# One attention step per FFN tile held back behind `p_packed @ w_in` in a fused attention and softplus-FFN kernel

## The chip, the core and the metric

The kernel runs on one core of one Trainium2 chip. The metric is the device time of one execution in microseconds (us), lower is better; a verdict rests on the median of several executions. The core has a matmul engine (PE, with its weight loads shown as PEld), VectorE (DVE), ScalarE (ACT), GpSimd (POOL) and a queue that issues transfers (SyncE, SP). Each works through its own instruction list, and they wait for one another by semaphores.

## The reference

Two attentions in a row for 8 batches and 8 heads, then an FFN over the 4608 tokens. `p` has 32 rows for each head, so the second attention has only 32 keys.

```python
def sm_attn(qq, kk, vv):
    s = scale * np.matmul(qq, kk.transpose(0, 1, 3, 2))
    s = s - np.max(s, axis=-1, keepdims=True)
    a = np.exp(s)
    a = a / (np.sum(a, axis=-1, keepdims=True) + 1e-09)
    return np.matmul(a, vv)
p_packed = sm_attn(p, k, v)
out = sm_attn(q, p_packed, p_packed)
...
h = x @ w_in
g = np.maximum(h, 0.0) + np.log1p(np.exp(-np.abs(h)))
return (g @ w_out).astype(np.float32)
```

Here batch and heads are 8 and 8, the sequence is 576, the head size 64, `w_in` is 512 x 2048 and `w_out` 2048 x 512. `x` is `out` with the heads side by side.

## The kernel before

Since `x` is (attention weights) @ `p_packed`, the kernel never forms `x`. It multiplies `p_packed` by `w_in` first (`make_m`, L535) and then applies the attention weights to that product (`gemm1`, L564). For each batch b the FFN runs over 16 **tiles** f of 128 columns of `d_ff`. Both FFN products are made from a high and a low half of each operand, in three matmuls (L579, L617).

The main loop (L717) takes one (b, f) at a time:

- `gemm1` of tile f: twelve matmuls (L580) into the two PSUM buffers `ph`;
- the softplus of tile f, spread out by a generator: on ACT the absolute value (L602), Exp (L604) and Ln (L605), on DVE max plus add (L607), which is what frees `ph` for the next `gemm1`, then the split into halves (L594, L595);
- `gemm2` of tile f - 2 (L618): four **token tiles** t = 0 to 3, three matmuls each, into the `acc` buffers;
- behind each token tile, steps of the attention of batch b + 1. A running sum `due` grows by `PACE` = 0.56 (0.62 in batch 1), and one step is made for each whole unit;
- in batch 0 only, also behind each token tile, pieces of a **conversion** that turns the 64-bit weights into 32 bits. One conversion is two ACT instructions (L200, L204), two on DVE (L206, L211) and an addition on POOL (L219); for `w_out` also a cast on ACT (L238) and a subtraction on DVE (L244);
- at the end of the tile, where the tile after next begins a new block of columns, `make_m` of that block: small matmuls (L543) into two PSUM banks `psm`, which ACT (L558) and DVE (L559) read out. A block is 256 columns in batch 0 (every second tile) and 512 in the other batches (every fourth).

The attention steps and `make_m` take their banks from the same pool, `ps_m`, which has two buffers used in turn. An attention step that writes a bank just ahead of `make_m` makes one of the two `psm` banks wait until that step's result is copied out: by L268 for a transposed piece of k or q (`transposed`, L257), by L309 for transposed attention weights (`a1_transposed`, L304). The first attention of the two first batches (`attention_first`, L370) transposes k and q on PE; from batch 2 on (`attention_next`, L445) DVE does it.

PE's instructions run in the order in which the code issues them. On ACT, DVE, POOL and SP the order is chosen by a scheduler when the program is built, from dependencies, priorities and estimated times; at run time each list is fixed.

```python
    PACE = 0.56
    ...
    PACE_FIRST = 0.62
```

Of the kernel before, what the change touches and what calls it, by code (L numbers as in the profile page):

```python
# [26 lines left out]
def pack_attention_then_softplus_ffn(  # L27
# [14 lines left out]
    P = 128  # L42
# [7 lines left out]
    NT = S // P  # L50
# [44 lines left out]
    def load_pack(bg, queues):  # L95

        t = cv.tile([PW, H, D], F32, tag="m", name=f"p_{bg}", bufs=1)
        for i in range(BG):
            queues[i % len(queues)].dma_start(
                t[i * J:(i + 1) * J], p[bg * BG + i].rearrange("h j d -> j h d")  # L100
            )
        return t

    def pack_transposed(bg, t):
        for o in range(0, H, HG):
            ps = bank(f"ppt_{bg}_{o}")
            for i in range(HG):
                nc.tensor.transpose(
                    ps[:D, i * PW:(i + 1) * PW], t[:, o + i, :], ident[:PW, :PW]
                )  # L110
            dst = pT[:, o:o + HG, :].rearrange("x h j -> x (h j)")
            nc.vector.tensor_copy(dst[:D], ps[:D, :HG * PW])
            nc.scalar.copy(dst[D:], ps[:D, :HG * PW])
# [401 lines left out]
    def attention(b):  # L515
        return attention_first(b) if b < FIRST else attention_next(b)

    def weights(b):

        at_h = work.tile([P, G, S], F32R, tag="at_h", name=f"at_h_{b}", bufs=1)  # L520
        at_l = work.tile([P, G, S], F32R, tag="at_l", name=f"at_l_{b}", bufs=1)
        res[b]["at"] = (at_h, at_l)
        for g in range(G):
            aT = res[b]["aT"][g]
            nc.scalar.copy(at_h[:, g, :], aT)  # L525
            nc.vector.tensor_tensor(  # L526
                at_l[:, g, :], aT, at_h[:, g, :].bitcast(F32), op=ALU.subtract
            )


    def m_cols(b):

        return MC if b else MC // 2
# [30 lines left out]
    def gemm1(b, f, res):  # L564

        n = m_cols(b)
        halves = res["m"][f * P // n]
        at_h, at_l = res["at"]
        phs = []
        for c in range(2):  # L570
            ph = ps_h.tile([P, 512], F32, tag="h", name=f"ph_{b}_{f}_{c}")
            phs.append(ph[:, :C])
            i = 0
            for g in range(G):
                mh, ml = halves[g * n // MC]
                o = g * n % MC + f * P % n
                ms = slice(o, o + P)
                cs = slice(c * C, (c + 1) * C)
                for x, y in ((mh, at_h), (mh, at_l), (ml, at_h)):  # L579
                    nc.tensor.matmul(  # L580
                        ph[:, :C], x[:, ms], y[:, g, cs],
                        start=(i == 0), stop=(i == 3 * G - 1),
                    )
                    i += 1
        return phs
# [11 lines left out]
    def softplus(b, f, hv, done):  # L597
        e = work.tile([P, S], F32, tag="e", name=f"e_{b}_{f}")
        es = [e[:, c * C:(c + 1) * C] for c in range(2)]
        spans = [e] if b == 0 else es  # L600
        for c in range(2):
            nc.scalar.activation(es[c], hv[c], AF.Abs)  # L602
            for x in spans[c:c + 1] if b else spans[:c]:
                nc.scalar.activation(x, x, AF.Exp, scale=-1.0)  # L604
                nc.scalar.activation(x, x, AF.Ln, bias=1.0)  # L605
        for c in range(2):
            nc.vector.scalar_tensor_tensor(es[c], hv[c], 0.0, es[c], op0=ALU.max, op1=ALU.add)  # L607
        yield
        yield
        r = (b % 2) * REST  # L610
        nc.gpsimd.tensor_copy(rest[:, rest_at(b, f), r:r + REST], e[:, NT * P:])  # L611
        yield
        done[b, f] = halves(f"{b}_{f}")
        split(*done[b, f], e[:, :NT * P])

    def gemm2_tile(acc, gh, gl, f, cs, first, last):
        for i, (x, y) in enumerate(((gh, wo_h), (gh, wo_l), (gl, wo_h))):  # L617
            nc.tensor.matmul(  # L618
                acc, x[:, cs], y[:, f, :],
                start=(first and i == 0), stop=(last and i == 2),  # L620
            )
# [73 lines left out]
    due = 0.0  # L695
# [19 lines left out]
    units = [(b, f) for b in range(B) for f in range(NF)]  # L715
    ahead, chain, due = iter(()), iter(()), 0.0
    for u in range(len(units) + LAG):  # L717
        if u < len(units):
            b, f = units[u]
            if f == 0:  # L720
                if (b + 1) % BG == 0 and b + 1 < B:
                    pack_transposed((b + 1) // BG, pt)
                ahead = attention(b + 1) if b + 1 < B else iter(())
                due = 0.0
            chain = softplus(b, f, gemm1(b, f, res[b]), gs)
            next(chain)
            if f == NF - 1:
                if (b + 2) % BG == 0 and b + 2 < B:
                    pt = load_pack((b + 2) // BG, (nc.sync,))
                for _ in ahead:  # L730
                    pass
                if b + 1 < B:
                    weights(b + 1)
        if u >= LAG:
            b2, f2 = units[u - LAG]
            gh, gl = gs.pop((b2, f2))
            if f2 == 0:
                acc = [ps_acc.tile([P, DM], F32, tag="acc", name=f"acc_{b2}_{t}") for t in range(NT)]
        last = u >= LAG and f2 == NF - 1 and b2 % 2 == 1
        if last:  # L740
            both = rests(b2)
            next(both)
        for t in range(NT):
            if u >= LAG:
                gemm2_tile(
                    acc[t], gh, gl, f2, slice(t * P, (t + 1) * P), f2 == 0, f2 == NF - 1
                )
                if f2 == NF - 1:
                    store(acc[t], [(0, b2, t * P, P)], f"{b2}_{t}", t)
            if u < len(units):  # L750
                due += PACE if b != FIRST - 1 else PACE_FIRST
                while due >= 1:
                    next(ahead, None)
                    due -= 1
                if b == 0:
                    cdue += CONV
                    while cdue >= 1:
                        next(conv, None)
                        cdue -= 1
            next(chain, None)  # L760
        if last:
            next(both)
        if u + 2 < len(units):


            nb, c = units[u + 2][0], units[u + 2][1] * P
            if c % m_cols(nb) == 0:
                make_m(nb, c // m_cols(nb), res[nb])
# [29 lines left out]
```

## Time and profile before

| what | value |
|---|---|
| median of 3 runs | 773.94 us (773.31 to 775.29) |
| the profiled execution | 774.48 us |
| its span in the trace | 772.7 us |
| PE busy | 729.3 us (94%), granted clock 0.985 on average |
| DVE busy | 527.4 us (68%) |
| ACT busy | 435.3 us (56%) |
| POOL busy | 99.0 us (13%) |

The three executions lie within 0.3% of one another. The profiled one lasted 1.8 us longer than its span, and 0.54 us longer than the median of the three. Busy time is the union of an engine's instructions; rows of the trace give a start, a duration, the engine, the source line, what is written and read, and in brackets how long the engine had stood still and what ended that.

### The profile page before, as it was taken

The page shows a single profiled execution, that of the slowest core. Times are in us where ns is not written, and L with a number is a line of the kernel's source. Part 1 is how long each engine was busy: PE and PEld are TensorE (multiplying, and loading weights), DVE is VectorE, ACT ScalarE, POOL GpSimd, SP SyncE. Part 2 cuts the span into 40 slices and gives each one's busy share as a digit, 9 for nine tenths or more (in the row PEclk, how much of TensorE's full clock was granted, in tenths as well). Part 3 has the DMA queues.
Part 4 walks back from the last instruction along what each step waited for, and adds up shares of the span by engine and source line. Part 5 has one row for each costly group of instructions (what it writes and reads, how often), then busy time and mean ns, then how long its engine had stood idle before and what let it go on. Part 6 is the DMA issues. An engine that isn't in the chain of part 4 may idle for free.

```text
span 772.7 us, 14153 instructions
## 1 busy us (share of the span) xinstructions
PE 729.3 (94%) x5360; PEld 577.0 (75%) x5360; DVE 527.4 (68%) x1092; ACT 435.3 (56%) x1057; POOL 99.0 (13%) x166
## 2 busy tenths in 40 slices
PE   6457997999999999999999999999999999999997
PEld 4346675687788778877887777878787777888886
DVE  2697869975877559575877559576877558565554
ACT  5667977666455445565555455565555355555540
POOL 1253434200000000000010000000010000000110
PEclk9969999999999999999999999999999999999999
DMA  9977644534302342052402332043401400010002
GB/s 205 247 194 179 180 133 125 120 74 78 76 17 68 63 68 57 1 116 47 87 0 69 62 63 62 1 98 51 92 1 55 75 2 1 1 55 1 1 1 68
DMA packets 149668, 55.97 MB, mean 72 GB/s; under 512 B 116320, under 2 KB 142944, under 8 KB 149600
## 3 DMA queue, kind: packets, MB, share of 16 engines
q1 hardware_dynamic: 149328, 55.00, 31.9%
q8 instruction: 42, 0.69, 0.4%
q14 instruction: 26, 0.21, 0.1%
q10 hardware_dynamic: 272, 0.07, 0.0%
HBM read 45.61 MB, written 9.44 MB: 71 GB/s over the span
## 4 chain that ended last, share of the span: by engine, by line
PE 82%; DVE 6%; ACT 6%; DMA 4%; POOL 1%; issue 1%; SPq 0%; ACTq 0%; DVEq 0%; POOLq 0%
PE acc L618 41%; PE ph L580 26%; PE acc_m L618 6%; PE psm L543 4%; PE ps L275 2%; DMA w_in_sb<-in_q 2%; PE psp L318 1%; PE psa L308 1%; DMA k<-in_k 1%; ACT m L200 1%; DVE at_l L526 1%; DVE t L211 1%; POOL t L219 1%; ACT e L604 1%; DVE t L206 1%
## 5 line engine op out<-in xcount | busy, mean ns | idle before, releaser
L602 ACT ACTIVATE e<-ph 128x288 f32<-128x288 f32 x256 | 103.1, 404 | 189.3 <-PE ph L580 142.4
L618 PE MATMUL acc<-wo_h,gh 128*128 128x512 f32 x512 | 207.6, 405 | 0.0
L607 DVE SCALAR_TENSOR_TENSOR e<-ph,e 128x288 f32<-128x288 f32 x256 | 113.3, 451 | 131.9 <-ACT e L605 128.2
L618 PE MATMUL acc<-wo_l,gh 128*128 128x512 f32 x512 | 200.9, 392 | 0.0
L618 PE MATMUL acc<-wo_h,gl 128*128 128x512 f32 x512 | 200.8, 392 | 0.0
L580 PE MATMUL ph<-at_h,mh 128*128 128x288 f32 x512 | 158.9, 310 | 14.8 <-ACT at_h L525 7.5
L580 PE MATMUL ph<-at_l,mh 128*128 128x288 f32 x512 | 153.3, 299 | 3.7 <-DVE at_l L526 3.7
L580 PE MATMUL ph<-at_h,ml 128*128 128x288 f32 x512 | 152.7, 298 | 0.0
L580 PEld LDWEIGHTS ph<-at_h,mh 128*128 128x128 f32 x512 | 97.6, 191 | 48.8 <-DVE e L607 10.8
L611 POOL COPY rest<-e 128x64 f32<-128x64 f32 x128 | 53.2, 416 | 575.8 <-DVE e L607 544.2
L618 PEld LDWEIGHTS acc<-wo_h,gh 128*128 128x128 f32 x512 | 96.2, 188 | 27.4 <-issue 10.2
L618 PEld LDWEIGHTS acc<-wo_h,gl 128*128 128x128 f32 x512 | 96.1, 188 | 21.0
L604 ACT ACTIVATE e<-e 128x288 f32<-128x288 f32 (+1 forms) x240 | 109.5, 456 | 3.9
L605 ACT ACTIVATE e<-e 128x288 f32<-128x288 f32 (+1 forms) x240 | 109.4, 456 | 3.2
L618 PEld LDWEIGHTS acc<-wo_l,gh 128*128 128x128 f32 x512 | 96.4, 188 | 13.0
L580 PEld LDWEIGHTS ph<-at_l,mh 128*128 128x128 f32 x512 | 97.8, 191 | 8.2 <-DVE at_l L526 5.3
L580 PEld LDWEIGHTS ph<-at_h,ml 128*128 128x128 f32 x512 | 97.8, 191 | 0.0
L595 DVE TENSOR_TENSOR gl<-e,gh 128x512 fp32r<-128x512 f32 x128 | 87.7, 685 | 5.5
L558 ACT CAST mh<-psm 128x512 fp32r<-128x512 f32 (+1 forms) x72 | 35.9, 540 | 53.5 <-PE psm L543 53.4
L594 DVE CAST gh<-e 128x512 fp32r<-128x512 f32 x128 | 55.5, 434 | 5.1
L559 DVE TENSOR_TENSOR ml<-psm,mh 128x512 fp32r<-128x512 f32 (+1 forms) x72 | 42.8, 623 | 20.2 <-ACT mh L558 19.6
L543 PE MATMUL psm<-w_in_sb,pt 64*32 64x512 f32 (+1 forms) x576 | 40.0, 560 | 9.7 <-ACT T_k L268 4.8
(79 smaller groups left out, 693.5 us busy)
## 6 DMA issues: line engine op xcount, KB each, us to landing
v<-in_v SPq DMA_DIRECT2D x16, 576.0 KB, 5.0
x_i<-in_moe_w_in SPq DMA_DIRECT2D x28, 256.0 KB, 4.5
k<-in_k SPq DMA_DIRECT2D x48, 144.0 KB, 3.1
q<-in_q SPq DMA_DIRECT2D x48, 144.0 KB, 3.2
x_o<-in_moe_w_out SPq DMA_DIRECT2D x11, 512.0 KB, 3.8
out<-o SPq DMA_DIRECT2D x18, 256.0 KB, 2.5
rest<-in_moe_w_out SPq DMA_DIRECT2D x5, 512.0 KB, 6.0
k<-in_k SPq DMA_DIRECT2D x4, 576.0 KB, 6.5
```

The lines of the kernel that those rows point to most:

```text
L543: nc.tensor.matmul(ps[hh * J:(hh + 1) * J, :n], res["pt"][g][o:o + D, hh * J:(hh + 1) * J], w_in_sb[o:o + D, hh, c * n:(c + 1) * n], start ...
L558: nc.scalar.copy(mh[:, cols], ps[:, :n])
L559: nc.vector.tensor_tensor(ml[:, cols], ps[:, :n], mh[:, cols].bitcast(F32), op=ALU.subtract)
L580: nc.tensor.matmul(ph[:, :C], x[:, ms], y[:, g, cs], start=(i == 0), stop=(i == 3 * G - 1),)
L594: nc.vector.tensor_copy(hi, x)
L595: nc.vector.tensor_tensor(lo, x, hi.bitcast(F32), op=ALU.subtract)
L602: nc.scalar.activation(es[c], hv[c], AF.Abs)
L604: nc.scalar.activation(x, x, AF.Exp, scale=-1.0)
L605: nc.scalar.activation(x, x, AF.Ln, bias=1.0)
L607: nc.vector.scalar_tensor_tensor(es[c], hv[c], 0.0, es[c], op0=ALU.max, op1=ALU.add)
L611: nc.gpsimd.tensor_copy(rest[:, rest_at(b, f), r:r + REST], e[:, NT * P:])
L618: nc.tensor.matmul(acc, x[:, cs], y[:, f, :], start=(first and i == 0), stop=(last and i == 2),)
```

## The change

One condition is added where the attention steps are made. `mf` is true when this tile will end in a `make_m`; then no step is made behind the last token tile (t = 3). The sum `due` keeps growing, so the step is made behind the first token tile of the next tile.

```diff
             if u < len(units):
                 due += PACE if b != FIRST - 1 else PACE_FIRST
-                while due >= 1:
+                mf = u + 2 < len(units) and units[u + 2][1] * P % m_cols(units[u + 2][0]) == 0
+                while due >= 1 and not (mf and t == NT - 1):
                     next(ahead, None)
                     due -= 1
```

Whether a step falls due at that place follows from the sums alone. In batch 0 it does at tiles 0, 4, 8 and 12 (of the eight tiles that end in `make_m`), and in batch 1 at tiles 2, 6, 10 and 14; of those in batch 1, two make nothing there (an empty step, and the end of the list). From batch 2 on the sum passes no whole number at t = 3 of such a tile, so no step moves. Four of the moved steps hold PE work: a transpose of k at tile 0, of attention weights at tile 4, of q at tile 8 (all in batch 0), and of attention weights at tile 6 of batch 1. No moved step issues a transfer of its own.

**PE, end of tile 0 of batch 0.** `ph_0_1` is the second half of `gemm1` of tile 0, `psT_k_0_0` and `psT_k_0_1` are transposes of k, `psm_1_0` and `psm_1_1` the two banks of `make_m`, `ph_1_0` is `gemm1` of tile 1. Before:

```order
L580 MATMUL ph_0_1_534<-at_h_521,ml_0_0_516 128x288
L262 MATMUL psT_k_0_0_551<-ident,k_0_497 128x96 x3
L262 MATMUL psT_k_0_1_573<-ident,k_0_497 128x96 x3
L543 MATMUL psm_1_0_587<-w_in_sb,pt_0_351 32x256 x4
L543 MATMUL psm_1_1_588<-w_in_sb,pt_1_428 32x256 x4
L580 MATMUL ph_1_0_603<-at_h_521,mh_0_0_515 128x288
```

After, to the transposes behind `gemm1` of tile 1:

```order
L262 MATMUL psT_k_0_0_551<-ident,k_0_497 128x96 x3
L543 MATMUL psm_1_0_581<-w_in_sb,pt_0_351 32x256 x4
L543 MATMUL psm_1_1_582<-w_in_sb,pt_1_428 32x256 x4
L580 MATMUL ph_1_0_597<-at_h_521,mh_0_0_515 128x288
...
L580 MATMUL ph_1_1_604<-at_h_521,ml_0_0_516 128x288
L262 MATMUL psT_k_0_1_618<-ident,k_0_497 128x96 x3
L262 MATMUL psT_k_0_2_634<-ident,k_0_497 128x96 x3
L262 MATMUL psT_k_0_3_649<-ident,k_0_497 128x96 x3
```

The second transpose of k went from ahead of `make_m` to behind the next `gemm1`; `psm_1_0` now takes the bank that this transpose had. At tiles 4 and 8 the move is the same, past `make_m`, `gemm1` and the first token tile of `gemm2`; at those three places and in batch 1 PE's order is otherwise what it was.

The lists of ACT and DVE differ in much more, though only in batch 0 (from 50 to 150 us of the trace of before): the scheduler chose other places for the conversions.

**ACT, tile 3 of batch 0.** `e_3` is the softplus of tile 3 (read from `ph`), `m_` and `r_` are the two instructions of a conversion, `T_k` a copy of transposed k. Before:

```order
L602 ACTIVATE e_3_782<-ph_3_1_775 128x288
L268 COPY T_k_1_1_798<-psT_k_1_1_794 128x288
L204 ACTIVATE r_745<-x_o_632 128x512
L200 ACTIVATE m_743<-x_o_632 128x512
L604 ACTIVATE e_3_782<-e_3_782 128x576
L204 ACTIVATE r_807<-x_o_661 128x512
L605 ACTIVATE e_3_782<-e_3_782 128x576
```

After:

```order
L602 ACTIVATE e_3_782<-ph_3_1_775 128x288
L604 ACTIVATE e_3_782<-e_3_782 128x576
L268 COPY T_k_1_1_798<-psT_k_1_1_794 128x288
L605 ACTIVATE e_3_782<-e_3_782 128x576
L200 ACTIVATE m_712<-rest 128x512
```

Three conversion instructions that stood between the absolute value and Ln of tile 3 now come later.

**ACT, tile 4 of batch 0.** `e_4` is the softplus of tile 4, `T_k_1_3` the last copy of k that the scores of batch 1's second head group need, `wo_h` a cast of converted `w_out`. Before:

```order
L602 ACTIVATE e_4_851<-ph_4_0_837 128x288
L602 ACTIVATE e_4_851<-ph_4_1_844 128x288
L604 ACTIVATE e_4_851<-e_4_851 128x576
L268 COPY T_k_1_3_865<-psT_k_1_3_861 128x288
L605 ACTIVATE e_4_851<-e_4_851 128x576
```

After:

```order
L602 ACTIVATE e_4_851<-ph_4_0_837 128x288
L200 ACTIVATE m_743<-x_o_632 128x512
L204 ACTIVATE r_807<-x_o_661 128x512
L602 ACTIVATE e_4_851<-ph_4_1_844 128x288
L604 ACTIVATE e_4_851<-e_4_851 128x576
L200 ACTIVATE m_805<-x_o_661 128x512
L238 CAST wo_h<-t_747 128x512
L605 ACTIVATE e_4_851<-e_4_851 128x576
L268 COPY T_k_1_3_865<-psT_k_1_3_861 128x288
```

The copy of k moved behind the conversion work of tile 3 and behind Ln.

Five more places of ACT's list are used below, told in words. In tile 5 the copies L309 of the two transposed halves of attention weights stood with the second one right behind Ln; now both stand behind Ln, and between them an L200, an L204 and the Exp of the first softmax (L295). In tile 10 the copy of transposed q stood behind the cast L238, now ahead of it. In tile 11 an L200, an L204 and a cast stood between Exp and Ln, now behind Ln. In tile 12 an L200 and an L204 (of the last block of `w_in` that batch 0 needs) moved from behind Ln to ahead of Exp, and the copy `T_q_1_3` from between Exp and Ln to behind Ln and one more L200. In tile 13 a cast stood between the two absolute values, now behind Ln. On SP some loads of k for batch 2 stand a few places later among the loads of weights.

## The prediction, made before the changed kernel ran

> **What bounds the kernel now.** I read the chain of work that ended last first, then PE's busy time in stretches, then the waits. A tile means an FFN tile of batch 0 unless said otherwise.
>
> ```profile
> PE 82%; DVE 6%; ACT 6%; DMA 4%; POOL 1%; issue 1%; SPq 0%; ACTq 0%; DVEq 0%; POOLq 0%
> ```
>
> PE is most of the chain, so what shortens the kernel is time in which PE stands still. The next view cuts the trace at the starts of `gemm1` of tiles 1, 3, 4, 5, 6, 8, 9, 11, 12, 13 and 14. The first number behind the window is its length, the second PE's busy time; PEclk is the clock granted, 1.00 being full.
>
> ```profile
> 45.90:53.85 7.95, 3.13 (x23) 1.27 (x21) 7.20 (x12) 6.03 (x12) 5.20 (x4) 0.71 0.70 194
> 68.32:75.37 7.05, 5.21 (x39) 4.24 (x31) 4.89 (x13) 7.05 (x17) 3.33 (x3) 1.00 0.84 220
> 75.37:82.90 7.53, 7.42 (x62) 4.68 (x62) 7.53 (x14) 6.39 (x16) 3.72 (x5) 1.00 0.91 229
> 82.90:88.69 5.79, 5.79 (x80) 4.80 (x76) 5.10 (x12) 5.26 (x12) 3.21 (x3) 1.00 0.45 151
> 101.14:109.13 7.99, 7.20 (x96) 5.21 (x94) 6.09 (x14) 5.39 (x12) 3.61 (x4) 1.00 0.50 132
> 109.13:121.94 12.81, 11.10 (x92) 8.45 (x88) 10.51 (x23) 9.03 (x18) 5.13 (x5) 1.00 0.56 148
> 121.94:128.82 6.88, 5.20 (x38) 4.23 (x31) 5.65 (x14) 6.42 (x14) 2.29 (x2) 1.00 0.43 116
> 128.82:136.84 8.02, 6.36 (x59) 4.28 (x59) 7.98 (x16) 4.75 (x9) 3.26 (x4) 1.00 0.42 118
> 136.84:142.11 5.27, 4.61 (x32) 3.77 (x24) 4.32 (x8) 3.91 (x9) 1.61 (x1) 1.00 0.33 54
> 142.11:772.70 630.59, 624.67 (x4468) 499.78 (x4468) 423.55 (x881) 333.05 (x844) 48.17 (x116) 1.00 0.24 49
> ```
>
> Length less busy time is what PE idles: 4.82 us ahead of tile 1, 1.84 in tile 3, 0.79 in tile 8, 1.71 in tiles 9 and 10, 1.68 in tile 11, 1.66 in tile 12, 0.66 in tile 13. Behind 142.11 PE is busy for 99%: a change acts there only by what it shifts. So the case is decided in batch 0, where the conversions fill ACT and DVE (ACT 7.05 of 7.05 us in tile 3, DVE 7.53 of 7.53 in tile 4).
>
> ```profile
> PE ph L580 <- DVE e L607: 7.2, 4, 3.0
> PE psm L543 <- ACT T_k L268: 4.8, 2, 4.5
> PE psm L543 <- ACT T_q L268: 2.5, 2, 1.7
> ```
>
> These are PE's three largest waits between 45.9 and 142.2 us (total, times, longest). The change aims at the second and third kind, but moves the scheduler's ACT list too, which decides the first.
>
> **The change part by part.** The four moved PE steps first; three lie where PE idles.
>
> ```profile
> 50.97 0.38 ACT L268 COPY T_k<-psT_k 128x288 f32<-128x288 f32 x1
> ...
> 51.49 1.07 PE L543 MATMUL psm<-w_in_sb,pt 64*32 64x256 f32 x8 [4.55 <-ACT T_k L268]
> 52.84 1.08 PE L543 MATMUL psm<-w_in_sb,pt 64*32 64x256 f32 x8 [0.27 <-ACT T_k L268]
> ```
>
> At tile 0 both `psm` banks wait for copies of k. Without the second transpose in front, the first `psm` runs in the 4.55 us that PE idles, but the second still needs the bank of the first transpose, whose copy L268 (50.97) keeps its place in ACT's list. So it starts at 51.49, not 52.84: **-1.35**, not -4.55. The transpose itself goes behind `gemm1` of tile 1, where PE waits for the softplus anyway (3.0 is the longest row above); that hides it, and if Ln came early it would cost the 0.5 or so of its matmuls.
>
> ```profile
> 67.73 0.66 PE L543 MATMUL psm<-w_in_sb,pt 64*32 64x256 f32 x16
> ...
> 81.24 0.53 PE L308 MATMUL psa<-ident,a 128*96 128x128 f32 x3
> 81.70 1.27 PE L543 MATMUL psm<-w_in_sb,pt 64*32 64x256 f32 x16
> ```
>
> At tile 4 the transpose held PE for 0.46 (81.24 to 81.70), and the `make_m` behind it took 1.20 to the start of `gemm1` (82.90), against 0.59 at 67.73 (to 68.32): it had waited for the transpose's copy. That is **-1.07**. At tile 8 the 0.79 goes and the transpose of q, some 0.3, too: **-1.1**. What they cost in their new place lies between nothing and the 0.46 here; I take 0.3 each, for tile 4 inside the wait of tile 5 below, for tile 8 as **+0.3**. The step of batch 1 only changes neighbours: nothing, at most 0.46 either way.
>
> Now ACT's list, walked with start-to-start times of these rows.
>
> ```profile
> 71.27 0.43 ACT L602 ACTIVATE e<-ph 128x288 f32<-128x288 f32 x1
> 71.56 0.43 ACT L268 COPY T_k<-psT_k 128x288 f32<-128x288 f32 x1
> 71.84 0.72 ACT L204 ACTIVATE r<-x_o 128x512 int32<-128x512 uint32 x1
> 72.40 0.71 ACT L200 ACTIVATE m<-x_o 128x512 f32<-128x512 f32 x1
> 72.98 0.71 ACT L604 ACTIVATE e<-e 128x576 f32<-128x576 f32 x1
> 73.55 0.70 ACT L204 ACTIVATE r<-x_o 128x512 int32<-128x512 uint32 x1
> 74.11 0.71 ACT L605 ACTIVATE e<-e 128x576 f32<-128x576 f32 x1
> ```
>
> A long ACT instruction takes about 0.57, a copy 0.29, an absolute value 0.3. In tile 3 three conversions leave the way from L602 to Ln: 1.7, and the 1.84 that PE waits goes as nothing else is late: **-1.8**. The work isn't gone; it stands in tile 4 now, ahead of the copy that the scores need.
>
> ```profile
> 78.30 0.38 ACT L268 COPY T_k<-psT_k 128x288 f32<-128x288 f32 x1
> ...
> 78.83 0.71 PE L275 MATMUL ps<-T_k,pT 64*32 64x288 f32 x16
> ```
>
> Today the copy starts 2.93 behind tile 4's start (75.37) and the scores 3.46. In the new list there stand ahead of it, from the first L602 (which `gemm1` allows at 1.1): two L602, four conversion and cast instructions, Exp and Ln, 0.6 and 6 x 0.57, and about 0.35 in which L204 waits for its buffer: 1.1 + 0.6 + 3.4 + 0.35 = 5.5, done at 5.85. PE waits from 3.5 to 5.85: **+2.3**, a new wait.
>
> ```profile
> 86.37 0.80 ACT L295 ACTIVATE a<-a,nm 128x576 f32<-128x576 f32 x1
> ...
> 87.70 0.46 ACT L309 COPY a1T<-psa 96x384 f32<-96x384 f32 x1
> ```
>
> In tile 5 the second copy L309 follows Ln, a first copy (0.4), L200, L204 and L295 (0.76). Absolute values done at 2.25 behind `gemm1`'s start, Exp, two conversions and Ln 2.3, then 0.4 + 1.14 + 0.76 + 0.4: 7.25. Today PE leaves for tile 6 at 5.79. The products that read the copy need 0.4 to 0.5 more, so tile 6 starts at 7.75: **+1.95**, the second new wait.
>
> Tile 10: the copy of q passes the cast, and the 1.71 goes: **-1.7**. Tile 11: three instructions leave the way to Ln, 1.7 against a wait of 1.68: **-1.7**. Tile 12: the conversion for the last `w_in` block comes about 2 earlier, so `make_m` doesn't wait for POOL: **-1.66**. But the copy `T_q_1_3` now stands behind two conversions, Exp, a third, Ln and a fourth.
>
> ```profile
> 131.75 0.38 ACT L268 COPY T_q<-psT_q 128x288 f32<-128x288 f32 x1
> ...
> 132.28 0.72 PE L275 MATMUL ps<-T_q,pt 64*32 64x288 f32 x16
> ```
>
> It started 2.93 behind tile 12's start (128.82); now 2.25 + 6 x 0.58 = 5.7, done at 6.1, while PE reaches the scores at 3.46 and does part of them: **+2.5**, the third new wait. Tile 13: the cast leaves the absolute values: **-0.66**.
>
> Last, the walk uses DVE's shortest times, and these rows speak against that.
>
> ```profile
> 77.31 1.60 POOL L219 TENSOR_TENSOR t<-t,r 128x512 int32<-128x512 int32 x1 [1.03 <-DVE t L211]
> ...
> 77.68 1.78 DVE L244 TENSOR_TENSOR wo_l<-t,wo_h 128x512 fp32r<-128x512 f32 x1
> ...
> 80.12 0.68 DVE L244 TENSOR_TENSOR wo_l<-t,wo_h 128x512 fp32r<-128x512 f32 x1
> ```
>
> The same subtraction takes 0.68 alone and 1.78 beside a POOL addition. In the new order a few DVE instructions that free `ph` (in tiles 11 and 13) fall beside one. Nothing to 2.2 (two such); I charge one: **+1.1**.
>
> [...]
>
> Sum: -1.35 - 1.07 - 1.1 + 0.3 - 1.8 + 2.3 + 1.95 - 1.7 - 1.7 - 1.66 + 2.5 - 0.66 + 1.1 = -2.9. The profiled execution took 774.48 us, so 771.6; it lies 0.54 above the median shown, so against that **771.1**.
>
> **The rivals.**
>
> - *New waits cover the gains.* The same walk with the two-instruction charge, and with one or two of the four gains in tiles 10 to 13 (1.7, 1.7, 1.66, 0.66) lost because another engine is late at the same place. For it: DVE is busy 7.98 of 8.02 us in tile 12. Against: in tile 11 it has 1.2 us to spare. -2.9 + 1.1 + 1.7 = -0.1: **773.8**.
> - *The new waits don't come.* The copies in tiles 4, 5 and 12 reach PE in time. For it: the scheduler placed them by its own estimate. Against: ACT is in order, and the counts above are of its list. -2.9 - 2.3 - 1.95 - 2.5 = -9.7: **764.3**.
> - *Slower: ACT's conversions sit in front of PE's copies.* The three new waits (6.75) and the 1.1 stand, and the gains in tiles 3 and 10 to 13 (7.5 together) don't come, since DVE or POOL, not ACT, ends those waits then. Direct moves -3.2, + 6.75 + 1.1 = +4.65: **778.6**. From the point where less than 0.62 of the 7.5 comes the kernel is slower than now, and below 0.31 by over 0.3%. Against it: the 1.84 and 1.68 rows name L607 behind an ACT list with conversions between.
> - *Hardly anything moves.* No step moves from batch 2 on, and all of it cancels: **773.9**.
>
> **How the numbers follow.** Forecast 0.50, waits that cover the gains 0.22, no new waits 0.14, slower 0.11, nothing 0.03. The predicted time is the forecast's, 771.1; its own range is 769.0 (no charge, and 1 of one wait less) to 773.2 (double charge, and 1 more). Runs of this kernel can tell about 0.3%, 2.3 us, from no change: the line is 771.6, just above the forecast, so of its 0.50 I give 0.32 to faster, 0.18 to the same. Faster: 0.32 + 0.14 = 0.46, and 0.02 of the covered case, 0.48. Same: 0.18 + 0.20 + 0.03 = 0.41. Slower 0.11. The range goes from 767.5 (half of the new waits absent, 3.4 less than the forecast) to 775.5 (a third of the way from now to the slower case); it leaves out over half of the case without new waits and most of the slower one, under 0.2 together.
>
> **What would show it.** In the trace of after: one `psm` ahead of tile 1 at once and the other behind the L268 near 51.4; no idle PE ahead of tile 4's `gemm1`; PE waiting about 2 us each for T_k ahead of L275 in tile 4, for a1T ahead of L318 in tile 5 and for T_q ahead of L275 in tile 12; `make_m` of tiles 8, 10 and 12 without waits. Tile 14 of batch 0 starting near 139 instead of 142.11, and from there to the end the same 630.6 us. I am wrong if that last stretch changes by more than 0.5 us, or if the three waits for copies are absent.

## The result: slower by 0.65%

| | changed | before |
|---|---|---|
| median | 780.25 us (779.93 to 780.78, 6 executions) | 774.65 us (773.31 to 778.87, 6 executions) |
| ratio | 1.0065, 95% interval 1.0052 to 1.0079 | |
| profiled execution | 780.11 us, span 778.3 | 774.48 us, span 772.7 |
| batch 0's first `gemm1` to batch 1's | 120.13 us | 114.57 us |

The forecast was 771.1, its range 767.5 to 775.5. The last row holds the whole loss: 5.56 us. It comes from PE's busy time in stretches, the kernel before and then the changed one (length; then busy time and count for PE, weight loads, DVE, ACT and POOL; then the granted clock, DMA share, GB/s):

```profile
38.71:153.28 114.57, 94.20 (x719) 70.35 (x719) 96.48 (x188) 86.26 (x177) 46.69 (x43) 0.92 0.62 156
153.28:772.70 619.42, 613.58 (x4396) 491.54 (x4396) 412.84 (x861) 325.06 (x828) 46.09 (x113) 1.00 0.23 47
```

```profile
39.24:159.37 120.13, 98.50 (x719) 71.33 (x719) 98.64 (x188) 86.42 (x177) 45.37 (x43) 0.88 0.59 149
159.37:778.30 618.93, 613.12 (x4396) 491.33 (x4396) 412.90 (x861) 324.64 (x828) 46.07 (x113) 1.00 0.23 47
```

Behind batch 0 hardly anything changed (619.42 and 618.93). Within it PE idles only 1.26 us more (21.63 against 20.37). The other 4.30 is busy time: the same 719 records of matmuls took 98.50 instead of 94.20, at a clock of 0.88 instead of 0.92.

### The profile page after: what moved, and what is told of

Same layout as the page of the kernel before. It is cut to its first block, busy times and chain, and to the rows that moved or that the text cites. A ratio compares the mean times of both kernels' runs of the same rounds, so it can differ in the third digit from the quotient of the medians.

```text
span 778.3 us, 14153 instructions
## 1 busy us (share of the span) xinstructions
PE 735.9 (95%) x5360; PEld 579.4 (74%) x5360; DVE 529.3 (68%) x1092; ACT 435.2 (56%) x1057; POOL 97.6 (13%) x166
## 4 chain that ended last, share of the span: by engine, by line
PE 83%; DVE 7%; ACT 5%; DMA 3%; issue 1%; POOL 1%; SPq 0%; ACTq 0%; POOLq 0%; DVEq 0%
PE acc L618 41%; PE ph L580 25%; PE acc_m L618 6%; PE psm L543 4%; PE ps L275 3%; DMA w_in_sb<-in_q 2%; PE psp L318 1%; PE psa L308 1%; DVE at_l L526 1%; DVE t L211 1%; ACT m L200 1%; ACT e L604 1%; DVE t L206 1%; ACT e L602 1%; POOL t L219 1%
## 5 line engine op out<-in xcount | busy, mean ns | idle before, releaser
L607 DVE SCALAR_TENSOR_TENSOR e<-ph,e 128x288 f32<-128x288 f32 x256 | 113.3, 452 | 130.8 <-ACT e L605 128.7
L611 POOL COPY rest<-e 128x64 f32<-128x64 f32 x128 | 51.7, 404 | 574.5 <-DVE e L607 545.7
L559 DVE TENSOR_TENSOR ml<-psm,mh 128x512 fp32r<-128x512 f32 (+1 forms) x72 | 42.7, 622 | 19.1 <-ACT mh L558 18.5
L543 PE MATMUL psm<-w_in_sb,pt 64*32 64x512 f32 (+1 forms) x576 | 40.6, 573 | 5.6 <-ACT T_k L268 3.8
```

The costliest lines, as they stand in the source:

```text
L543: nc.tensor.matmul(ps[hh * J:(hh + 1) * J, :n], res["pt"][g][o:o + D, hh * J:(hh + 1) * J], w_in_sb[o:o + D, hh, c * n:(c + 1) * n], start ...
L559: nc.vector.tensor_tensor(ml[:, cols], ps[:, :n], mh[:, cols].bitcast(F32), op=ALU.subtract)
```

## The profile after, by tiles

The same view by tiles, for tiles 3, 4, 5, 9, 11, 12 and 13 of batch 0. Before they took 7.05, 7.53, 5.79, 5.48, 6.88, 8.02 and 5.27 us, all at 1.00. (The edges of the windows of tiles 9, 11 and 12 are rounded by up to 0.1 us; by the starts of `gemm1` these tiles took 8.02, 6.93 and 10.34.)

```profile
67.20:72.24 5.04, 5.04 (x38) 4.42 (x31) 3.13 (x9) 4.96 (x12) 1.29 (x1) 1.00 0.46 153
72.24:83.04 10.80, 7.89 (x61) 4.62 (x59) 7.99 (x15) 8.14 (x17) 4.95 (x5) 0.89 0.89 232
83.04:91.39 8.35, 6.70 (x87) 5.53 (x79) 6.11 (x14) 6.49 (x14) 3.25 (x4) 0.94 0.20 68
111.70:119.80 8.10, 6.06 (x51) 4.38 (x47) 6.20 (x11) 5.51 (x12) 1.98 (x2) 1.00 0.39 100
126.00:132.84 6.84, 5.43 (x30) 3.99 (x31) 6.06 (x13) 6.37 (x14) 1.77 (x3) 1.00 0.30 79
132.84:143.20 10.36, 8.36 (x60) 5.16 (x60) 9.73 (x17) 5.10 (x10) 4.78 (x5) 0.84 0.59 146
143.20:148.59 5.39, 4.58 (x32) 3.74 (x25) 5.39 (x10) 4.85 (x11) 1.29 (x1) 1.00 0.17 35
```

Tile 3 lost its wait, as walked: tile 4 starts at 72.24, 3.1 earlier than before. Tile 4 alone then loses 3.3. PE's rows with a wait in front of 0.8 us or more from tile 3 on, same kernel (the bracket says how long PE stood still and what ended that):

```profile
79.19 0.70 PE L275 MATMUL ps<-T_k,pT 64*32 64x288 f32 x10 [2.91 <-ACT T_k L268]
90.91 0.54 PE L318 MATMUL psp<-v,a1T 96*32 96x64 f32 x24 [1.66 <-ACT a1T L309]
98.77 0.64 PE L543 MATMUL psm<-w_in_sb,pt 64*32 64x256 f32 x8 [1.56 <-ACT a1T L309]
116.32 0.47 PE L262 MATMUL psT_q<-ident,q 96*128 96x96 f32 x3 [2.04 <-DVE ml L559]
132.84 0.40 PE L580 MATMUL ph<-at_h,mh 128*128 128x288 f32 x1 [1.40 <-DVE e L607]
138.99 1.20 PE L275 MATMUL ps<-T_q,pt 64*32 64x288 f32 x10 [2.00 <-ACT T_q L268]
148.59 0.40 PE L580 MATMUL ph<-at_h,mh 128*128 128x288 f32 x1 [0.81 <-DVE e L607]
```

The first, second and sixth are the three waits of the prediction (2.3, 1.95 and 2.5 there). The third, fourth and fifth are not in it as costs, and the seventh was to go. The last row of L275 takes 1.20 where the first takes 0.70: it ran on a slower clock. Half-microsecond windows behind the first wait show that:

```profile
80.00:80.50 0.50, 0.50 (x3) 0.41 (x3) 0.05 (x1) 0.29 (x2) 0.50 (x2) 1.00 0.98 370
80.50:81.00 0.50, 0.50 (x3) 0.38 (x2) 0.00 (x0) 0.50 (x1) 0.14 (x1) 0.64 1.13 320
...
83.50:84.00 0.50, 0.50 (x4) 0.50 (x4) 0.50 (x2) 0.29 (x2) 0.00 (x0) 0.50 0.00 0
84.00:84.50 0.50, 0.50 (x5) 0.50 (x5) 0.50 (x2) 0.00 (x0) 0.00 (x0) 0.95 0.00 0
```

About 1.4 us after the wait ends the clock falls to 0.50 and stays there for 3.4 us (some 80.6 to 84.0), which is 1.7 us less work. At the wait of 2.00 in tile 12, which ends at 138.99, the same happens from 138.7 to 142.1; there the clock falls 0.3 us before the wait ends. Between 64 and 770 us the profiled execution of the kernel before has no such stretch. That is in part luck: run e9 below has the same wait ahead of tile 4 as the kernel before (1.83 and 1.84 us), and there the clock fell (0.81 over the tile).

The waits that end with DVE have one thing in common. DVE ahead of the transposes of tile 9, ahead of tile 12 and ahead of tile 14, same kernel, and last ACT's Ln of tile 11 and POOL's three additions beside them:

```profile
114.17 1.76 DVE L244 TENSOR_TENSOR wo_l<-t,wo_h 128x512 fp32r<-128x512 f32 x1
115.85 0.74 DVE L559 TENSOR_TENSOR ml<-psm,mh 128x256 fp32r<-128x256 f32 x2
...
130.09 1.24 DVE L361 TENSOR_SCALAR z<-z 128x18 f32<-128x18 f32 x1
131.36 0.27 DVE L362 RECIPROCAL z<-z 128x18 f32<-128x18 f32 x1
131.66 0.76 DVE L363 TENSOR_TENSOR a<-a,z 128x576 f32<-128x576 f32 x1
132.34 0.45 DVE L607 SCALAR_TENSOR_TENSOR e<-ph,e 128x288 f32<-128x288 f32 x1
...
146.34 1.82 DVE L352 TENSOR_TENSOR a<-a,m 128x576 f32<-128x576 f32 x1
148.09 0.81 DVE L607 SCALAR_TENSOR_TENSOR e<-ph,e 128x288 f32<-128x288 f32 x2
```

```profile
130.10 0.69 ACT L605 ACTIVATE e<-e 128x576 f32<-128x576 f32 x1
```

```profile
113.82 1.55 POOL L219 TENSOR_TENSOR w_in_sb<-t,r 128x512 int32<-128x512 int32 x1 [2.61 <-ACT e L602]
130.01 1.28 POOL L219 TENSOR_TENSOR t<-t,r 128x512 int32<-128x512 int32 x1 [3.42 <-ACT e L604]
146.26 1.29 POOL L219 TENSOR_TENSOR t<-t,r 128x512 int32<-128x512 int32 x1 [3.59 <-DVE t L211]
```

In tile 11 Ln ended at 130.8, but L607, which frees `ph`, began at 132.34: ACT was early, and DVE stood in the softmax division. At each of the three places the DVE instruction just ahead runs beside an addition of POOL. The same instructions took 0.16 (L361) and 0.75 (L352) at these places of the kernel before, where no addition of POOL runs beside them; its rows are these:

```profile
126.88 0.16 DVE L361 TENSOR_SCALAR z<-z 128x18 f32<-128x18 f32 x1
...
140.47 0.75 DVE L352 TENSOR_TENSOR a<-a,m 128x576 f32<-128x576 f32 x1
```

With 0.68 for L244 where POOL stands still (at 143.54 of the changed kernel), the three took 1.08, 1.08 and 1.07 us longer beside an addition. The prediction's 0.68 (at 80.12 of the kernel before) ran beside a copy of POOL, L611, so the rows speak of additions only; the cause of the lengthening is not shown.

## The experiments

Four theories were put to the test. **A**: what PE waits for stands behind conversions in ACT's list, and the waits are the loss. **B**: the half clock behind the waits is a cost of its own. **C**: the moved PE steps cost something in their new place. **D**: DVE and POOL, not ACT, end some of the waits, so gains that ACT's list promises don't come.

"Stretch" is the time from batch 0's first `gemm1` to batch 1's, in the profiled execution (before 114.57, changed 120.13); "half clock" are the tiles in which it begins behind 64 us (that of the last 10 us of the span left out). Both come from one execution of each run, and executions of one kernel differ: the mean clock of those of the kernel before ran from 0.966 to 0.990. So between kernels the medians decide. The kernel before was timed anew beside each group.

| run | median us | beside it, before | ratio, 95% | stretch | half clock |
|---|---|---|---|---|---|
| e4 tile 0 only | 776.30 | 775.64 | 1.0009 (0.9997 to 1.0021) | 115.80 | 4 |
| e7 tile 4 only | 777.86 | 775.70 | 1.0035 (1.0023 to 1.0047) | 118.05 | 12, 14 |
| e6 tile 8 only | 777.81 | 775.70 | 1.0035 (1.0021 to 1.0049) | 117.98 | 10, 14 |
| e8 batch 1 only | 775.30 | 775.70 | 0.9998 (0.9983 to 1.0012) | 114.58 | none |
| e2 changed, copies first | 779.13 | 775.64 | 1.0048 (1.0031 to 1.0064) | 118.08 | 9 |
| e3 before, copies first | 777.53 | 775.64 | 1.0023 (1.0009 to 1.0036) | 117.87 | 12, 14 |
| e1 changed, 2 waits filled | 779.65 | 775.64 | 1.0048 (1.0030 to 1.0066) | 119.70 | 6 |
| e5 changed, 4 waits filled | 778.82 | 775.70 | 1.0046 (1.0030 to 1.0062) | 118.42 | none |
| e10 changed, from tile 0 on | 778.18 | 775.06 | 1.0030 (1.0015 to 1.0044) | 118.59 | 9 |
| e11 tile 0 only, filled | 774.83 | 775.06 | 0.9995 (0.9985 to 1.0004) | 114.90 | 8 |
| e9 before, filled | 773.10 | 775.06 | 0.9973 (0.9959 to 0.9987) | 113.80 | 4 |
| e15 before, filled, tile 3 too | 772.72 | 774.96 | 0.9965 (0.9952 to 0.9977) | 112.56 | 13 |
| e12 transposes of tile 9 later | 779.45 | 775.06 | 1.0050 (1.0034 to 1.0067) | 119.33 | 7, 12 |
| e13 division behind L607 | 780.11 | 774.96 | 1.0060 (1.0044 to 1.0075) | 121.07 | 4, 7 |
| e14 all mends | 775.57 | 774.96 | 1.0002 (0.9993 to 1.0011) | 115.43 | none |

### One place at a time (e4, e7, e6, e8)

```diff
-                mf = ... == 0
+                mf = ... == 0 and u == 0
```

with `u == 0` in e4, `u == 4` in e7, `u == 8` in e6 and `u >= 12` in e8.

> Only the step of tile 0 of batch 0 is held back; tiles 4, 8, 12 and batch 1 as before. ACT's list up to tile 4 is then that of the changed kernel, with the copy T_k_1_3 behind four conversion instructions and Ln; in tile 5 it is near that of before. Theory A with B: tile 4 starts about 3 earlier than before, then PE waits 2.9 for T_k and runs 3.4 us at half clock, and the lead is gone by tile 5; no wait for a1T in tile 5; 774 to 776. Theory A without B: 772.5. If the loss of the changed kernel came from the steps of tiles 4 and 8 themselves (C), this kernel is faster than before by 2 or more.

> Only the transposed attention weights of tile 4 are held back; up to tile 4 ACT's list is that of before. PE's order: tile 4's end 1.07 shorter. ACT's list in tile 5: the second copy L309 stands behind Ln, an L200 and the softmax Exp, as in the changed kernel: a wait for a1T of 1.7 and none for T_k in tile 4. Theory A: batch 1 starts 0.5 to 1.5 later than before (153.3), 775 to 776; no half clock behind 64 us if no single wait is over 2. Theory of the prediction without new waits: 773.

> Only the transpose of q of tile 8 is held back; up to tile 8 everything is as before. Prediction's step: psm at the end of tile 8 doesn't wait (-0.8 and -0.3), the transpose costs 0.3 in tile 9, and the scheduler's new list brings the T_q wait of 2.0 in tile 12 but frees psm in tiles 10 and 12 (-1.7 each): together 773 to 774 by the same sums. Theory C (the moved transpose waits for the bank that make_m now holds, as in the changed kernel: 2.04 for DVE's L559): tile 9 grows by 2 or more over before (5.48), 776 to 777.

> The condition from tile 12 on alone: only the transposed attention weights of tile 6 of batch 1 move on PE, and batch 0 is that of before on all engines. All theories: within 0.3% of before (774.6), batch 0 as before to 0.3 us; if it is slower by 1 or more, the loss has a part in batch 1 that the trace of the changed kernel doesn't show.

e8 takes the time of the kernel before: batch 1 has no part in the loss. e4 has the wait of 2.91 for T_k in tile 4 and one half clock behind it, and still loses only 1.2 in the stretch: it idles 17.91 us in it where before idles 20.37, and runs 3.69 busier. e6 shows B most plainly. Its idle time is that of before (20.49), tile 8 became 1.6 shorter and tile 9 0.4 longer, yet the stretch is 3.4 longer. Its windows of tiles 11 and 14, at a lower clock:

```profile
121.80:129.20 7.40, 6.52 (x35) 5.55 (x31) 5.99 (x14) 5.84 (x13) 1.63 (x2) 0.80 0.34 80
144.40:151.50 7.10, 7.06 (x40) 5.29 (x40) 5.96 (x13) 2.19 (x4) 0.47 (x2) 0.76 0.76 163
```

So C fails in e6 (tile 9 took 5.85, no wait for L559), and holds only together with the list that the whole change brings. Tiles 4 and 8 each cost what half the change costs; tile 0 costs nothing that can be measured.

e7 was slow for another reason than expected. The wait for a1T ahead of its L318 in tile 5 was 0.36, not 1.7; its long waits are 2.39 for POOL's L219 in tile 12 and 2.29 for L607 ahead of tile 14, and a half clock begins at each (0.95 over tile 12 and 0.76 over tile 14). In e6 the wait for T_q in tile 12 was 0.94 where 2.0 was expected, and a wait of 2.72 for L607 came ahead of tile 14. So each single move brings waits of its own, at places that a walk of the whole change's lists doesn't give.

### Copies ahead of conversions (e2, e3)

```diff
-        nc.scalar.copy(dst, ps[:, :C])
+        with tc.high_priority(offset=FRONT if b == 1 else 0):
+            nc.scalar.copy(dst, ps[:, :C])
```

and the same around the copy L309. PE's list stays that of the changed kernel (e2) or of the one before (e3).

> The changed kernel, with the copies L268 and L309 of batch 1's attention given priority over the conversions on ACT; PE's order is that of the changed kernel. Theory A (the new waits come from conversions in front of the copies, and the moves on PE gain): the waits for T_k in tile 4, a1T in tiles 5 and 6 and T_q in tile 12 (2.9, 1.7, 1.6, 2.0) fall under 0.5 each, the clock stays 1.00 in tiles 4 and 12, and the time is 770.5 (780.25 less 7 of waits and 3 of clock), so faster than before by about 4. Theory D (DVE and POOL hold the same places, the gains can't come): the waits for copies go but waits for DVE (e, ml) take their place, and the time is 774 to 777. Theory C (the moved PE steps cost by themselves): slower than the kernel before with the same priority by 1 or more.

> The kernel before with the same priority for the copies L268 and L309 of batch 1's attention: the control of the run above. Theory A: the psm waits for T_k and T_q behind tiles 0, 8 and 12 that the change aims at stay or shrink, and the time is 772 to 774.7; the changed kernel with the same priority is 2 to 3 faster than this one. Theory C: this one is the faster of the two.

The waits for copies shrank as A has it, T_k from 2.91 to 1.20, and those for a1T and T_q at the named places went. Others came. PE's waits of e2 from tile 4 on (total, times, longest; its lines from L269 on are one or two higher):

```profile
PE ph L582 <- DVE e L609: 4.9, 4, 2.2
PE psa L309 <- DVE ml L561: 2.2, 2, 1.9
PE psm L545 <- DVE pp L328: 1.7, 1, 1.7
PE psm L545 <- ACT T_q L269: 1.6, 1, 1.6
PE ps L276 <- ACT T_k L269: 1.2, 1, 1.2
```

That is D in its mechanism: three of the five end with DVE. The time of e2, 779.13, lies above the 774 to 777 of D, and that of e3, 777.53, above the 772 to 774.7 of A. The control, e3, became 3.3 longer by the same priority. Under one rule for ACT the two orders of PE differ by 0.2 us in the stretch (118.08 and 117.87), but the profiled execution of e2 was its fastest (776.55). By the medians the changed order is 1.6 slower, as C had it, with intervals that overlap. So under this rule the moves on PE win nothing, against what A expected. This is no test of PE's order alone: the scheduler made two sets of lists here too, and those of ACT and DVE differ between e2 and e3 in many places of batch 0. A alone is refuted as a way to win, not as the cause of the waits.

### Filling the waits (e1, e5, e10, e9, e15, e11)

Matmuls that nobody reads are put where PE would wait, into columns of a bank that nobody reads; every other list stays as it is.

```diff
+    def keep_busy(ps, n):
+
+        if not n:
+            return
+        w = res[0]["at"][0].bitcast(F32)
+        cols = ps.shape[-1]
+        for _ in range(n):
+            nc.tensor.matmul(ps, w[:, 0, :J], w[:, 0, :cols], start=True, stop=True)
...
+            if hh == HG - 1:
+                keep_busy(ps[hh * J:, :C], {(1, 1, 1, 0): 5, (2, 1, 1, 0): 3}.get((nm, b, g, c), 0))
```

This is a part of e10; e1 has the same matmuls in tiles 4 and 12, written as a loop in place. e5 adds three ahead of L318 in tile 5 and three between the two `psm` of tile 6; e10 adds five between the two `psm` of tile 0 and two behind the second transpose of k, now in tile 1. In the kernel before, e9 puts eight behind the second transpose of k (tile 0) and six behind the fourth (tile 1), e15 three more in tile 3. e11 is e4 with tiles 0, 1, 4 and 6 filled.

> The changed kernel, with five more fp32 matmuls (128x32 weights, 288 columns) ahead of the last head's scores in tile 4 and three in tile 12, where PE waits 2.9 and 2.0 us for the copies of k and q; every other instruction list is unchanged. Theory B (the two waits are followed by 3.4 us each at half the granted clock, and that costs time on top of the wait): the clock stays 1.00 behind both waits, the scores and make_m behind them take their usual 0.7 and 0.6 us, and the kernel takes 777.0 (3.2 less than 780.25; 778.5 if only one wait is covered). Theory A (only the waits cost, not the clock): the clock may rise, but what follows waits for ACT or DVE anyway, and the time is 780.3 within 0.5. If the added matmuls don't count as activity for the clock, the clock still falls to 0.5 and the time is 780.3: then nothing is told.

> As the first run with matmuls that fill waits, and three more each ahead of the products that wait for a1T in tile 5 and between the two psm banks in tile 6 (where the first run's low clock had moved to). Theory B (cold clock is a cost of its own, and the first run only moved one of its two cold stretches): no stretch at half clock behind 64 us, batch 1 starts 2.5 to 3.4 earlier than in the changed kernel (156 to 157 against 159.4), time 777. Theory A (ACT and DVE set the pace, PE's clock is hidden): no cold stretch, but batch 1 starts within 0.8 of the changed kernel (158.6 or later), 779.5 to 780.3.

> The changed kernel with waits filled in tiles 0, 1, 4, 5, 6 and 12; all other lists unchanged. The fifth run's kernel still had PE at half clock from 38 to 57 and 60 to 64 us. Theory B: no half clock behind 51, batch 1 starts another 1.5 to 3 us earlier than in the fifth run (118.4 behind the start of the first product of batch 0 there, 115.4 to 117 here), 776. Theory A: within 0.7 of the fifth run (778.8).

> The kernel before with matmuls that only fill PE's two longest waits of batch 0 (eight behind the second transpose of k in tile 0, six behind the fourth in tile 1); all other lists unchanged. In the kernel before PE runs at half clock from 50 to 57 us and from 60.2 to 63.6 us. Theory B (half clock is a cost of its own): tile 2 shrinks from 7.68 by 1.7, tile 1 by up to 1, batch 1 starts 1.5 to 2.7 earlier (150.6 to 151.8 against 153.3), 773 against 775.7: a version better than both. Theory A (ACT and DVE set the pace of batch 0): the clock rises, but the wait for the softplus of tile 3 grows from 1.84 by as much, and the time stays within 0.5 of before.

> The kernel before with matmuls that fill the waits of tiles 0 and 1 (as in the ninth run) and three more in tile 3, behind whose wait of 1.83 the half clock had moved in the ninth run (tile 4 took 9.00 instead of 7.53). Theory B: no half clock behind 50, tile 4 back at 7.5, batch 1 starts at 112.3 behind batch 0's first product (113.8 in the ninth run, 114.57 before): 771.7 where before is 775.1. If the half clock moves on again to another wait, 773.1 as in the ninth run.

> The kernel that holds back the step of tile 0 only, with waits filled in tiles 0, 1, 4 and 6. It idled 17.9 us from the start of batch 0's products to batch 1's, against 20.4 in the kernel before, but PE's busy time was 3.7 longer. Theory B: with the clock up the stretch is 115.80 less 1.7 (tile 4) less 1.7 (tile 2) = 112.4, against 114.57 before: 773.5 where before is 775.7, better than both kernels. Theory A: 115.3 or more, 775.5 to 776.

In e1 tile 4 ran at 1.00 and took 9.81 instead of 10.80, and tile 12 took 8.96 instead of 10.34. But the half clock came back behind another wait, of 1.55 in tile 6, and the median was 779.65, not 777.0. The windows of tile 4 and of that place, and the row with the wait (L549 is L543 here):

```profile
72.22:82.03 9.81, 9.44 (x71) 5.37 (x69) 6.99 (x13) 7.63 (x17) 4.95 (x5) 1.00 1.00 249
97.60:101.00 3.40, 3.40 (x20) 3.04 (x13) 2.55 (x6) 1.95 (x4) 1.79 (x1) 0.52 0.84 223
```

```profile
97.30 0.73 PE L549 MATMUL psm<-w_in_sb,pt 64*32 64x256 f32 x8 [1.55 <-ACT a1T L315]
```

e5 has none behind 64 us:

```profile
39.55:157.97 118.42, 102.59 (x747) 72.63 (x747) 98.77 (x188) 86.37 (x177) 45.32 (x43) 0.91 0.62 151
```

The stretch is 1.71 shorter than the changed kernel's, half of the two times 1.7 that the half clock took. The other half is given back, some 0.9 of it ahead of tile 14, where the wait for L607 grew from 0.81 to 1.69. So in these two executions B is right, at **1.7 us**, and 3.85 of the 5.56 stay when no clock falls. The medians of the changed kernel don't show it clear of noise: 1.0046 (1.0030 to 1.0062) in e5 beside 1.0065 (1.0052 to 1.0079) without the added matmuls.

In the kernel before the gain of such filling stayed, and there the medians show it (0.9973 and 0.9965, both intervals below 1): tile 2 fell from 7.68 to 6.29, tiles 0 and 1 by 0.4 each, and no wait behind them grew in e9, which still had a half clock in tile 4. e15 fills the wait of tile 3 ahead of it too (its half clock came in tile 13), and beats both kernels: 772.72 beside 774.96. Its tile 2, and the stretch:

```profile
37.80:150.40 112.60, 100.09 (x753) 73.11 (x753) 96.48 (x188) 86.17 (x177) 46.78 (x43) 0.94 0.65 159
58.92:65.21 6.29, 6.29 (x59) 4.29 (x59) 5.64 (x12) 4.44 (x10) 1.89 (x3) 1.00 0.73 171
```

e10 and e11 came out less well than B expected. The half clock moved once more, to waits that had not been filled (tiles 9 and 8). And in e11 tile 4 won nothing for B: at a clock of 1.00 it took 11.77 where e4 took 11.96, tile 5 took 6.93 instead of 6.38, and waits of 0.64 and 0.81 for a1T stood there instead. There ACT set the pace, as A has it.

### Tile 9 and tile 11 (e12, e13, e14)

```diff
-                while due >= 1 and not (mf and t == NT - 1):
+                while due >= 1 and not (mf and t == NT - 1 or u == 9 and t < 2):
```

is e12. In e13 the division depends on the softplus of its tile (`newest[0]` is `e`):

```diff
+        if (b, g) == (1, 0):
+            nc.vector.scalar_tensor_tensor(
+                zf, newest[0][:, C:C + S // J], 0.0, zf, op0=ALU.mult, op1=ALU.add
+            )
         nc.vector.tensor_scalar_add(zf, zf, 1e-9)
```

e14 has both, and the filled waits of e10.

> The changed kernel with the two transposes of q of tile 9 made behind the third token tile instead of behind the first and second; a few instructions of DVE and ACT in tiles 9 and 13 change places with it. Theory C for tile 9 (the moved transpose waits 2.04 for the bank that make_m holds until DVE's L559): the wait falls to 0.7 or less and tile 9 from 8.02 to 6.7; batch 1 starts 1.3 earlier than 159.4 unless it is given back; 779. If DVE and ACT set the pace there (D), tile 9 loses its wait and tiles 10 and 11 grow by as much: 780.3.

> The changed kernel, where in tile 11 DVE's division of the second softmax (L361 to L363) is made to depend on the softplus of that tile (zero times 18 of its elements is added to the sums, one small instruction more), so that the two L607 stand ahead of it; some conversions of tiles 11 and 12 change places on DVE and ACT. Theory D (the gain of tile 11 was taken by this division in front of L607, not by ACT): the wait of 1.40 ahead of tile 12's first product goes, tile 11 falls from 6.93 to 5.6, and batch 1 starts 1 to 1.4 earlier than in the changed kernel (118.8 behind the start of batch 0's first product, against 120.13); 779. If ACT set that place, the wait stays over 1 and the time is 780.3.

> The changed kernel with three mends together: waits filled in tiles 0, 1, 4, 5, 6 and 12, the transposes of tile 9 behind its third token tile, and the division of tile 11 behind L607. If the loss is the sum of its places, the stretch from batch 0's first product to batch 1's is 118.6 (the tenth run) less 1.5 (its stretch at half clock in tile 9) less 1.3 (tile 9's wait) less 1.3 (tile 11) = 114.5, that of the kernel before (114.57), and the time is that of before, 775. If DVE and ACT are full and each mend is given back, it stays at 116.5 or more, 777.

In e12 the wait of tile 9 fell to 0.69 and the tile to 6.71, and nothing of it was given back in tiles 10 and 11 (0.5 was, in tile 13): C holds for tile 9 as the whole change makes it. In e13 the wait ahead of tile 12 went and tile 11 took 5.41 instead of 6.93, so DVE, not ACT, had kept that gain: D. But tile 13 grew by 0.9, and in that execution the half clock fell on tiles 4 and 7, with a wait of 3.09 ahead; the stretch was longer and the time the same within its interval. Alone the mend can't be told from none, nor can that of e12 by its median (1.0050, 1.0034 to 1.0067). Since e13 puts L607 ahead of the whole division, it doesn't separate the division's place in the list from the 1.08 by which L361 took longer beside POOL's addition.

Together, in e14, the mends bring the stretch to 115.43 (114.5 expected) and the time to that of before, 1.0002 (0.9993 to 1.0011). That doesn't make the found places the whole loss, for e14 also fills the waits of tiles 0 and 1, where no loss came from. Cut at the start of tile 3, the kernel before, the changed one and e14:

```profile
38.71:68.32 29.61, 18.72 (x111) 13.66 (x111) 24.60 (x41) 18.86 (x38) 13.19 (x11) 0.69 0.72 176
68.32:153.28 84.96, 75.48 (x616) 56.68 (x608) 71.88 (x149) 67.40 (x140) 33.51 (x32) 1.00 0.59 149
```

```profile
39.24:67.20 27.96, 19.04 (x111) 13.25 (x111) 24.46 (x40) 18.49 (x38) 13.25 (x11) 0.63 0.76 187
67.20:159.37 92.17, 79.46 (x616) 58.08 (x608) 74.18 (x148) 67.93 (x140) 32.12 (x32) 0.96 0.53 138
```

```profile
37.77:63.73 25.96, 19.90 (x126) 12.14 (x126) 24.84 (x40) 17.75 (x37) 13.28 (x11) 0.80 0.87 202
63.73:153.20 89.47, 83.98 (x643) 59.53 (x635) 73.37 (x150) 68.72 (x141) 32.28 (x32) 1.00 0.57 142
```

The change wins 1.65 up to the start of tile 3 and loses 7.21 from there on. Of these 7.21 the mends take back 2.7, and the other 2.0 that e14 wins come from tiles 0 to 2. Against the kernel before with tiles 0 and 1 filled as well (e9, 773.10) e14 is 2.5 slower. From tile 3 on e14 is still 4.5 longer than the kernel before: its tiles 4, 5 and 12 are 2.7, 2.1 and 2.0 longer, for there the three copies still come late and the waits are only filled.

## Why the prediction was wrong

**What held.** Batch 0 decides: the stretch from tile 14 on was 629.7 against 630.6. That is shorter by 0.9 where the prediction allowed 0.5, a sign of being wrong by its own words, but it is not where the loss lies. The moves of tile 0 (-1.35; tile 0 became 1.45 shorter), of tile 4's end (-1.07; -1.04 in e12, with the clock at 1.00) and of tile 8's end (-1.1; tiles 7 and 8 together -0.98), tile 3 (-1.8; -2.01), the psm waits of tiles 10 and 12 (-1.7, the tile got 1.2 shorter; -1.66, gone) and batch 1 (nothing) are as walked. The three new waits were 2.91, 1.66 and 2.00, together 6.6 against 6.75.

**The steps that failed**, by size:

- *The clock.* The sum put waits of 2 us and more into tiles whose clock was 1.00 and left it there. Two stretches at half clock came, 3.4 us in the trace; filling the waits won 1.7 of it in e5. Executions differ here too, with a mean clock of 0.971 to 0.979 in the changed kernel. The table of the prediction had the warning: 0.71 in the one window with a long wait, 4.82 us.
- *Tile 8's transpose in its new place, +0.3.* It waited 2.04, because the bank it takes is held until DVE's L559, and DVE had a split and an L244 of 1.76, beside an addition of POOL, in front. Row: 116.32. Shown by e12.
- *Tile 11, -1.7, and tile 13, -0.66.* Only ACT's list was walked. DVE's list had the division and the subtraction of the softmax in front of L607. Waits of 1.40 and 0.81 stayed. Shown for tile 11 by e13, though not how much of it was the L361 of 1.24 beside POOL's addition; for tile 13 it is read from the rows alone.
- *The charge for DVE beside POOL, +1.1.* The lengthening came and its size was not right: three DVE instructions in front of what PE waits for took 1.07 or 1.08 longer beside an addition, where one was charged and two were the upper end.
- *Tile 6.* A wait for a1T grew from 0.67 to 1.56; the walk of ACT's list went from tile 5 on to tile 10.

With 1.7 for the clock, 1.7 for tile 9, 1.4 and 0.8 for tiles 11 and 13 less the 1.1 charged, 0.9 for tile 6 and 0.5 for tile 10, that is 5.9 of the 8.5 us between -2.9 and +5.6; with the whole 3.4 of the clock it is 7.6. The rest is not assigned to a step, and the experiments don't show that the sizes add up.

**The rival** that said slower (778.6) had its chance too low at 0.11. Its mechanism came in half: the new waits stood, and of the five gains that it denied, those of tiles 11 and 13 did not come, for the reason it gave. That its +4.65 comes near the measured +5.6 is luck: of the 7.5 us of gains that it denied, 2.4 (tiles 11 and 13) failed to come, and it had neither the clock nor the waits of tiles 6 and 9. The rival by which the new waits don't come is refuted. What is open: how the changed order of PE alone would do under the lists of the kernel before. The scheduler makes those lists anew with each order, and it wasn't tried; e2 against e3 is the nearest to it, with lists that differ too. Open too is what removing the three waits for copies would win, since e2, which moved the copies ahead, brought other waits.

## What to carry to other kernels

A wait added to a busy engine can cost more than its length: here waits of 2.91 and 2.00 came with 3.41 us each at a clock of 0.50, and filling the waits won 1.7 us in e5. Put a term for it into the sum, and look in the trace at what followed the longest waits that are there. When a scheduler remakes the lists, walk every list that ends at the waiting instruction, DVE's as well as ACT's, and count what stands beside an addition of POOL (1.07 or 1.08 us longer here). Test a small reordering against a control in which the rest of the order is made by the same rule; here neither order of PE beat the kernel before that way. And give each mend its control: filling waits made the kernel before faster too, so a mended kernel that is level with the unmended one before has not shown that its loss is found.

## What the runs showed of the hardware

Beside some waits of PE the granted clock fell to 0.50. In the changed kernel's trace it was 0.50 from 60.16 to 63.57, from 80.64 to 84.05 and from 138.66 to 142.07, 3.41 us each time, and 1.00 between these and behind them up to 770. The length of one wait doesn't tell whether a fall comes: 1.55 (tile 6 of e1) and 1.83 (ahead of tile 4 in e9) had one behind them, 2.71 (ahead of tile 4 in e3) had none. Two waits of 0.52 and 1.34 in tile 8 had one behind them in e11 (rows of the next `gemm1` of 0.44 us) and none in e4 (0.29). What decides it is not shown.

Two kernels with the same instructions up to tile 9 had the same wait of 2.91 in tile 4. In the changed kernel the half clock followed in that tile (0.89 over it); in e12 tile 4 ran at 1.00, and it came only in tile 7 (0.75):

```profile
98.00:104.70 6.70, 6.65 (x33) 5.61 (x29) 3.16 (x9) 5.06 (x10) 3.08 (x2) 0.75 0.59 169
```

Tiles 4 and 5 took 10.80 and 8.35 us with it and 9.77 and 7.90 without, so here one such stretch cost 1.5 us.

In e10 a wait of 2.03 in tile 9 was followed by it (the tile's clock 0.82); in the changed kernel the 2.04 at that place was not (1.00).

With matmuls with weights of 32 columns in the wait, tile 4 of e1 ran at 1.00, against 0.89 in the changed kernel; e12 had 1.00 there without them, so one execution of each doesn't show that they keep the clock up. Those of e15 in the kernel before brought 0.35% (0.9965) by work that computes nothing, with a clock of 0.94 over the stretch where before had 0.92.
